# Softmax maxima sent out by halves of the queries, and the work of the last head pair laid out anew, in a DFT and attention kernel

## The chip, the cores and the metric

The kernel runs on one core of a Trainium2 chip. The metric is the device time of one execution in microseconds (us), the median of several runs. Inside the core, TensorE (PE) multiplies matrices, with weights loaded beside it (PEld); VectorE (DVE), ScalarE (ACT) and GpSimd (POOL) work elementwise and reduce; SyncE (SP) issues nearly all DMA transfers, in order.

## The reference

Two layers read the same input x of 2048 tokens by 640 features, and a gate of one number per token mixes them.

```python
a = x @ dft_hid_re.T ; b = x @ dft_hid_im.T
y = dft_seq_re @ a - dft_seq_im @ b                     # Fourier mixing
q = heads(x @ wq) ; k = x @ wk ; v = x @ wv             # 32 heads of 20, one k and v for all
p = softmax(q @ k.T * 20**-0.5)
o = (p @ v) @ wo
g = sigmoid((x * gate_w).sum(-1, keepdims=True))
out = g * y + (1 - g) * o
```

## The kernel before, in words

All operands are float32. Where accuracy asks for it an operand is split into a high and a low part and multiplied in three matmuls. The order on PE, ACT, DVE and POOL is the order in which the program issues (line 50, `manual_schedule`); SP's transfers are ordered by the framework.

**First stages (to 233 us).** q, k, v and the gate are projected. Then `x @ dft_hid` (line 137, tile `ab`) runs; its results `both` are stored to `x_d` in DRAM, while the first scores are already made. The operand tiles of this stage lie in two pools on the right side of SBUF, `w2` (the weights) and `x2` (inputs, `half`, `both`); both are closed before the main loop, whose pools (`cp`, `xp`, `pp` with the `pt` tiles, `op`) take their place.

**Attention.** Heads go in 16 pairs; each head of a pair uses one half of PE's rows, so two score matmuls of different halves run at the same time. Every score is made twice. An *a* score (line 353, 128 queries by 512 keys) serves the row maximum: DVE reduces it (line 360, tile `mx`). When the 64 units of a pair are done, `a_reduce` (line 366) and `a_final` (lines 374 to 376) reduce, transpose and split the maxima; they go to DRAM (`m_d`) and come back as rows 60 and 61 of each half of the query operand `qs`, where they subtract the maximum inside the matmul. A *b* score (line 811, 128 keys by 512 queries) uses that operand; ACT takes the exponential from PSUM into one of 16 `pt` tiles (line 821). An AV step (line 825, tile `av`) multiplies four `pt` tiles with the values; it fills all rows of PE. A b score of a pair needs that pair's maxima; a pair's b scores go by halves of the queries (`qh`), 16 key blocks each.

**DFT over the sequence.** One level of Strassen: 7 products, each of 8 blocks, 56 blocks in all; a block is 48 matmuls on each half of the rows (line 682, tile `y`, 320 columns). The matrix tiles are loaded as `craw` (1 MB for two), added where the product asks for it and split into `ch` and `cl` (lines 482 to 487, POOL, for the last blocks DVE). A block that ends is evicted by ACT (`y_evict`, line 711), then POOL adds it to earlier parts kept in `y_d`.

**The order by hand.** The string `PLAN`, *the list* below, is the main loop, one character for each step: `0` or `1` is a DFT matmul on that half of the rows; `a` to `f` and `A` to `F` are a scores of the pair's first and second head, and `g` to `l` and `G` to `L` b scores, where the letter names one of six PSUM banks; `V` is an AV step and `-` a DFT eviction. A score must wait until ACT or DVE has emptied its bank. The list holds 1,888 a scores (160 more came before it), 1,920 b scores, 4,608 DFT matmuls (48 blocks, accumulated in one bank, `GMAIN`, line 457) and 478 AV steps. `tick` (line 392) counts score pairs and starts what `later` set down.

**The last pair.** The loop from line 1025 on has 16 steps `kk`. Each runs 24 pairs of DFT matmuls, both halves at once into two banks, and four pairs of b scores of the last pair in a rotation of five banks; odd steps end with four AV steps (the first and the last step with two). Eight blocks are done there, each ending at the end of an odd step. Between the steps stand loads for the last stage (`BEFORE`: `load_wo` in steps 1 to 5).

**The end.** `o @ wo`, gated and added to y, from 1668 us on.

Of the kernel before, what the change touches and what calls it, by code (L numbers as in the profile page):

```python
# [34 lines left out]
def kernel(  # L35
# [46 lines left out]
    m_d = dram.tile([NPAIR, P, 2, 32], F32, name="m_d")  # L82
# [279 lines left out]
    mxr = {}  # L362

    def a_reduce(p):
        mxr[p] = sml.tile([P, 2 * NT], F32, name="mxr")
        nc.vector.tensor_reduce(
            mxr[p], mx.pop(p).rearrange("p h q c -> p (h q) c"), axis=AX.X, op=ALU.max
        )

    def a_final(p):  # L370

        mt = sml.tile([P, 32], F32, name="mt")
        ms = sml.tile([P, 2, 32], F32R, name="ms")
        nc.vector.transpose(mt, mxr.pop(p))
        nc.gpsimd.tensor_copy(ms[:, 0], mt)
        nc.gpsimd.tensor_tensor(ms[:, 1], mt, ms[:, 0].bitcast(F32), op=ALU.subtract)
        move(m_d[p], ms)

        m_v = m_d[p].rearrange("(g h b) i t -> h i b g t", g=4, h=2)
        for hh in range(2):  # L380
# [76 lines left out]
    GMAIN = LAST * NT // 5  # L457
# [3 lines left out]
    def load_c(g, sh):  # L461

        if g < len(GROUPS):
            n, k = GROUPS[g]
            c_raw[g, sh] = []
            for q, (i, th) in enumerate(PRODUCTS[n][0][::2]):
# [4 lines left out]
                move(raw, (cre, cim)[i][th * SJ + k, sh])  # L471
                c_raw[g, sh].append(raw)

    def split_c(g, sh):
        if g < len(GROUPS):
# [4 lines left out]
            eng = nc.vector if g > GMAIN else nc.gpsimd  # L480
# [387 lines left out]
    def finish_last(ts, sm):  # L868
# [20 lines left out]
        "B0A00K00F00CBjVV1e1g11d11l1c11h1e11a1j111f1h111c1-kJVHa1l1e11c1d11h11a1l11k1VHcDlAeVVCh1d1l11g1e11h1"
        "1c1l11d11gVHe0I0F00G0D00B0VIeGfDhVVhE0I0A00F00J000H0E00I00A0J000F0H00K00C0A00J0B00L00E0I000D0A000L0B"  # L890
        "iVVElj11c1g11b1l11e11d11i11g11h1l1e11c1-VdEaHcLVVDh1e1l11g1c11h111d1l11k1a111c1h11d111l1k1a1Hc1VLdKh"
        "AcVVfH0D0K00G0I00B00F0K00D0VVkAH00C00L0J00E0G00B00C00L00E0J000B00G0F00I00J00E00A0B0I00lDVVKc1a1l11h1"
        "1d1k11c1f11a111h11d1k11i1-VVBfKaIjVBk1i1f11j1a11k11h11c11l11d11a11k11h1c1f11d11KgVHkCfGdVVB00K00G0C0"
        "0L00D0B0K00G00I0F0D000E00B0A00LiVVDlI00E00H00A0L0J000C00E0H00A0L000C0D00BkVVFgIk1d111b1g11f11c1j111k"
        "1h111a1f11j1V-CaKbJlVk11c1j11a11l1h11e11c1d1GlV1e1h11c1g11d1l11e11b1iGVD0fIeB0A0VVJc0L0E000H0G00D00I"
        "00F0K00B0DgVVF00I00B0K00G0D00F00I00H0E00G00J00C0F00B0E000G0iJV1l1a11h1c11j11e11f1g11b1iDVVeGiFhJVe11"
        "fAi1b11j1-VIej11l11a111b1i1e111j1a1l11h11c1j11k11l1a11b1VcJaKlBVVdL0I0E00A0H00L00D0I00K0VViB0K0A0F00"
        "J00I00H00E0A000J0F0I00K00H00D00A000I0F00E0D00B0gCVV1f1g11e1j11b1i111l1a11k11d11i1h11f-AVVdKfIaHVdK1f"
        "1i11h11a11k1d1i11l111b1g11e1d11i11f1h111aKViDfBkAVViD00K0F00H0G00C0D00K0F000B0IaVViEJ00F0H00G00C0E00"
        "J0F00H000I00A000J0E00H0F00I00A0D00kHVVFh1c1g11e1j11b111l1a11i1j111e1l11h1VaE-cJfHVVaJ1e1h11i1l11d1g1"  # L900
        "11b11k1c1d111l1b11a111i11e1LjVIlBaDeVVlC0B0G00J0E0F00C00G0H00D0VVkA00L0B00I00D0Eg0L000B00I0D00G00K0F"
        "00C0H00G000J0K00F00B0CaVVj11f11k1b11i11a11j11lk111i11b1d11-GfVVKbIgDlVbKi11d11a11l1k11b11i1j111f1a11"
        "1k11b1i11d11l1eGVbDcFaKVVhED00I00L00A0H00E000I0J00L00B0A000I0E000J0H00F0aIVVjEF00H0A00I000J0E00H0F00"
# [99 lines left out]
    for what in PLAN:  # L1003
# [112 lines left out]
```

## Time and profile before

| | us |
|---|---|
| median of 3 runs | 1742.17 (1739.02 to 1743.29) |
| profiled execution | 1741.15 |
| its span, first to last instruction | 1739.4 |
| PE busy | 1727.9 |
| DVE busy | 1430.5 |
| ACT busy | 1195.5 |
| POOL busy | 815.4 |

The profile is of one execution. A row of a timeline has the start, the length, the engine, the line, the operation with tile written and tile read, the shapes and how many are merged; in brackets the idle time before it and what ended it. The ends of matmuls are modelled, so two lengths overlap; distances between starts are the safer reading. The chain of waits is followed back from the last instruction. A row of the windows has, for each engine, busy time and count, then the granted clock of PE as a share of full speed, the share of the DMA engines and GB/s.

### The profile page before, as it was taken

What the parts mean: (1) busy time and instruction counts of PE and PEld (TensorE: products, weight loads), DVE (VectorE), ACT (ScalarE), POOL (GpSimd) and SP (SyncE); (2) the same over time, 40 slices, a digit from 0 to 9 for tenths busy, and PEclk for the clock granted to TensorE, in tenths of its full rate; (3) what the DMA queues carried; (4) which work ended last, traced back from release to release, by engine and by line L of the source; (5) the groups of instructions that cost most, each with busy time, mean ns of one, the idle gap of its engine ahead of it and who ended that gap; (6) DMA issues with size and microseconds to landing.
All of it is one profiled execution on the core that took longest, in us unless ns stands there. A gap on an engine that the chain in (4) does not pass through costs nothing.

```text
span 1739.4 us, 40768 instructions
## 1 busy us (share of the span) xinstructions
PE 1727.9 (99%) x16342; PEld 1216.3 (70%) x16342; DVE 1430.5 (82%) x2355; ACT 1195.5 (69%) x2337; POOL 815.4 (47%) x559
## 2 busy tenths in 40 slices
PE   9999999999999999999999999999999999999999
PEld 8899976666666666666666666666666666667789
DVE  5779988888888898888898888889888898864254
ACT  4722257777777777777777777777777777777741
POOL 1012136554546464656666565565664344551242
PEclk9999999999999999999999999999999999999999
DMA  8873334243443442534544544253434233225667
GB/s 291 239 198 100 117 109 132 89 144 92 130 135 125 121 129 96 174 112 147 159 138 134 158 128 137 89 164 107 144 122 134 91 114 96 91 93 173 202 216 240
DMA packets 131002, 243.88 MB, mean 140 GB/s; under 512 B 26356, under 2 KB 77556, under 8 KB 128292
## 3 DMA queue, kind: packets, MB, share of 16 engines
q1 hardware_dynamic: 130012, 238.00, 43.6%
q0 software_dynamic: 800, 3.28, 0.6%
q8 instruction: 128, 2.10, 0.5%
q14 instruction: 62, 0.51, 0.1%
HBM read 194.62 MB, written 50.86 MB: 141 GB/s over the span
## 4 chain that ended last, share of the span: by engine, by line
PE 97%; DVE 1%; DMA 1%; ACT 0%; SPq 0%; issue 0%; ACTq 0%; DVEq 0%
PE av L825 28%; PE y L682 21%; PE b L811 17%; PE a L353 17%; PE ab L137 7%; PE o L126 1%; PE q L126 1%; PE q L128 1%; PE o L128 1%; PE o L127 1%; PE q L127 1%; DVE mx L360 1%; DMA x_d<-both 1%; DMA wqraw<-in_wq_dram 0%; PE kv L230 0%; PE kv L231 0%
## 5 line engine op out<-in xcount | busy, mean ns | idle before, releaser
L360 DVE TENSOR_REDUCE mx<-a 128x1 f32<-128x512 f32 x2048 | 1260.3, 681 | 159.4 <-PE a L353 101.4
L821 ACT ACTIVATE pt<-b 128x512 f32<-128x512 f32 x2048 | 1049.9, 621 | 319.4 <-PE b L811 191.1
L682 PE MATMUL y<-x,ch 64*128 64x320 f32 x3584 | 729.9, 304 | 1.1 <-ACT yt L711 1.1
L353 PE MATMUL a<-ks,qs 60*128 60x512 f32 x2048 | 723.2, 414 | 0.3 <-DVE mx L360 0.2
L811 PE MATMUL b<-qs,ks 62*128 62x512 f32 x2048 | 697.3, 415 | 2.0 <-ACT pt L821 1.7
L682 PEld LDWEIGHTS y<-x,ch 64*128 64x128 f32 x3584 | 551.2, 186 | 21.6 <-issue 10.5
L682 PE MATMUL y<-x,cl 64*128 64x320 f32 x1792 | 508.8, 304 | 0.0
L825 PE MATMUL av<-pt,vsb 128*32 128x512 f32 x4096 | 503.4, 600 | 0.0
L353 PEld LDWEIGHTS a<-ks,qs 60*128 60x128 f32 x2048 | 351.2, 185 | 140.2 <-DVE mx L360 102.5
L811 PEld LDWEIGHTS b<-qs,ks 62*128 62x128 f32 x2048 | 341.4, 185 | 141.7 <-ACT pt L821 72.7
L482 POOL TENSOR_TENSOR craw<-craw 128x1024 f32<-128x1024 f32 x80 | 189.4, 2368 | 267.0 <-DMA craw<-in_cre_dram 116.6
L682 PEld LDWEIGHTS y<-x,cl 64*128 64x128 f32 x1792 | 310.6, 186 | 3.5 <-issue 2.5
L825 PEld LDWEIGHTS av<-pt,vsb 128*32 128x32 f32 x4096 | 106.2, 109 | 194.6 <-issue 174.0
L487 POOL TENSOR_TENSOR cl<-craw,ch 128x1024 fp32r<-128x1024 f32 x98 | 231.9, 2367 | 7.8
L486 POOL CAST ch<-craw 128x1024 fp32r<-128x1024 f32 x98 | 101.6, 1037 | 142.2 <-PE y L682 113.6
L137 PE MATMUL ab<-wh,xh 64*128 64x320 f32 x640 | 126.6, 297 | 2.2 <-DVE both L557 1.8
L137 PE MATMUL ab<-wl,xh 64*128 64x320 f32 x640 | 126.2, 296 | 0.0
L137 PE MATMUL ab<-wh,xl 64*128 64x320 f32 x640 | 126.1, 296 | 0.0
L738 POOL TENSOR_TENSOR ya<-yt,ya 128x320 f32<-128x320 f32 x64 | 59.5, 946 | 97.8 <-ACT yt L711 93.9
L556 ACT ACTIVATE half<-ab 128x320 f32<-128x320 f32 x64 | 27.9, 436 | 104.1 <-PE ab L137 98.5
L137 PEld LDWEIGHTS ab<-wh,xl 64*128 64x128 f32 x640 | 92.9, 185 | 0.0
L137 PEld LDWEIGHTS ab<-wl,xh 64*128 64x128 f32 x640 | 92.9, 186 | 0.0
(88 smaller groups left out, 1083.3 us busy)
## 6 DMA issues: line engine op xcount, KB each, us to landing
craw<-in_cre_dram SPq DMA_DIRECT2D x96, 512.0 KB
craw<-in_cim_dram SPq DMA_DIRECT2D x96, 512.0 KB
xr<-x_d SPq DMA_DIRECT2D x88, 320.0 KB
qs<-qh_d SPq DMA_DIRECT2D x64, 160.0 KB
x_d<-both SPq DMA_DIRECT2D x64, 160.0 KB
ya<-y_d SPq DMA_DIRECT2D x64, 160.0 KB
y_d<-ya SPq DMA_DIRECT2D x64, 160.0 KB
xr<-in_xT_dram SPq DMA_DIRECT2D x20, 256.0 KB
```

Source lines behind the costliest of these rows:

```text
L126: nc.tensor.matmul(ps, wh, woven(xh), start=(i == 0), stop=False)
L137: nc.tensor.matmul(ps, w[r], woven(x[r]), start=(i == 0 and k == 0), stop=(i == n - 1 and k == 2))
L353: nc.tensor.matmul(ps, qs[p][b : b + 60, qb * P : (qb + 1) * P], woven(ks[b : b + 60, c * ROW : (c + 1) * ROW]), start=True, stop=True,)
L360: return nc.vector.tensor_reduce(mx[p][:, hh, qb, c : c + 1], ps, axis=AX.X, op=ALU.max)
L482: eng.tensor_tensor(raw, raw, raws[1], op=PRODUCTS[n][0][1])
L486: eng.tensor_copy(h, raw)
L487: eng.tensor_tensor(l, raw, h.bitcast(F32), op=ALU.subtract)
L682: mm = nc.tensor.matmul(ps[g % len(ps)], w, woven(x), start=start, stop=stop)
L738: nc.gpsimd.tensor_tensor(ya, yt, ya, op=how)
L811: nc.tensor.matmul(ps, ks[b : b + 62, kc * P : (kc + 1) * P], woven(qs[p][b : b + 62, qc * ROW : (qc + 1) * ROW]), start=True, stop=True,)
L821: halves.scored(nc.scalar.activation(t, ps, AF.Exp, scale=SCALE), n)
L825: nc.tensor.matmul(ps[32 * g : 32 * g + 32, :], vsb[:, kc, :], t, start=first, stop=last)
```

## The change

- **Maxima by halves.** `a_reduce` and `a_final` run after each 32 units, for 1024 queries, and send that half out: 32 stores to `m_d` in place of 16, and 128 loads into `qs` of half the size in place of 64. For the last pair the split is done by DVE in place of POOL.
- **The last half in the last pair.** The list ends with 32 units (64 a scores) left; steps 0 to 6 of the loop run them (`AS`), mixed with the b scores in the same five banks.
- **One more DFT block in the list** (`GMAIN` 49): 4,704 DFT matmuls there, 336 pairs in the loop, spread by `YS` over the steps; evictions come where a block of 48 pairs ends. c splits of four more blocks stay on POOL.
- **List, pools, load.** The list is another order, with 1,824 a scores, 1,920 b scores, 478 AV steps. Pool `x2` is allocated ahead of `w2`. The load of the first block's second half of c is issued by ACT. `load_wo` moves from steps 1 to 5 to steps 7 to 11.

```diff
-    m_d = dram.tile([NPAIR, P, 2, 32], F32, name="m_d")
+    m_d = dram.tile([2 * NPAIR, P, 2, 32], F32, name="m_d")
...
+    x2 = cw.enter_context(tc.tile_pool(name="x2", bufs=2, side="right"))
     w2 = cw.enter_context(tc.tile_pool(name="w2", bufs=1, side="right"))
-    x2 = cw.enter_context(tc.tile_pool(name="x2", bufs=2, side="right"))
...
-    mxr = {}
-
-    def a_reduce(p):
-        mxr[p] = sml.tile([P, 2 * NT], F32, name="mxr")
+    mxr = sml.tile([P, 2 * NT], F32, name="mxr", bufs=1)
+    nc.vector.memset(mxr, 0.0)
+
+    def a_reduce(p, f):
+
+        r = slice(SJ * f, SJ * f + SJ)
         nc.vector.tensor_reduce(
-            mxr[p], mx.pop(p).rearrange("p h q c -> p (h q) c"), axis=AX.X, op=ALU.max
+            mxr.rearrange("p (h q) -> p h q", h=2)[:, :, r], mx[p][:, :, r], axis=AX.X, op=ALU.max
         )
-    def a_final(p):
+    def a_final(p, f):
...
-        nc.vector.transpose(mt, mxr.pop(p))
-        nc.gpsimd.tensor_copy(ms[:, 0], mt)
-        nc.gpsimd.tensor_tensor(ms[:, 1], mt, ms[:, 0].bitcast(F32), op=ALU.subtract)
-        move(m_d[p], ms)
+        eng = nc.vector if p == LAST else nc.gpsimd
+        nc.vector.transpose(mt, mxr)
+        eng.tensor_copy(ms[:, 0], mt)
+        eng.tensor_tensor(ms[:, 1], mt, ms[:, 0].bitcast(F32), op=ALU.subtract)
+        m_p = m_d[2 * p + f]
+        move(m_p, ms)
...
+                move(row[:, r], m_v[hh, i : i + 1, r])
...
-        if u % 64 == 63:
-            later(1, a_reduce, u // 64)
-            later(2, a_final, u // 64)
+        if u % 32 == 31:
+            later(1, a_reduce, u // 64, u // 32 % 2)
+            later(2, a_final, u // 64, u // 32 % 2)
...
-    GMAIN = LAST * NT // 5
+    GMAIN = LAST * NT // 5 + 1
+    AMAIN = NA - 32
...
-                move(raw, (cre, cim)[i][th * SJ + k, sh])
+                move(raw, (cre, cim)[i][th * SJ + k, sh], nc.scalar if (g, sh) == (0, 1) else nc.sync)
...
-            eng = nc.vector if g > GMAIN else nc.gpsimd
+            eng = nc.vector if g > GMAIN + 3 else nc.gpsimd
...
-        "1aH1Id1k11f1a11h1111id1El11h1111i1g1Df1hKVDiG0B0F000KC00J00G0B00K0000F00J0C00gE0H00dFVVg11cHeD1lVgC0"
...
-        "0JkVVi11g11h1k11lJi1VVVj11i11g11111J11I11-"
...
+        "f1111k11c111j11gb111e1l1dVV00D0KF0000HA0I00J0E00000L000BI000G0J0E0000LB0C0V0F0BCjeG0VG0B0000ID0F000E"
...
+        "0H0000G0L00KH00I00G0000J0L0000000KHVVk1l11j111h1g111ik11VVVkiG11h1J111111I-"
...
-        **{kk: (lambda c=kk - 1: load_wo((c,)),) for kk in range(1, 1 + KC)},
+        **{kk: (lambda c=kk - 7: load_wo((c,)),) for kk in range(7, 7 + KC)},
...
-                if min(state) >= NA and sum(taken["b"]) % 2 == 0:
+                if min(state) >= AMAIN and sum(taken["b"]) % 2 == 0:
                     tick()
...
+    pairs = 0
+    AS = [5] * 6 + [2] + [0] * 9
+    YS = [19] * 7 + [23] * 5 + [22] * 4
     for kk in range(NT):
         block = 2 if kk in (0, NT - 1) else 4 * (kk % 2)
-        at = (1, 5, 9, 13) if block else (0, 6, 12, 18)
-        for i in range(24):
-            if i in at:
-                tick()
+        todo_s = sorted([((k + 0.25) / 4, 0) for k in range(4)] + [((k + 0.7) / AS[kk], 1) for k in range(AS[kk])])
+        span = YS[kk] - 6 if block else YS[kk]
+        for i in range(YS[kk]):
+            while todo_s and todo_s[0][0] * span <= i:
+                kind = todo_s.pop(0)[1]
+                if kind == 0:
+                    tick()
                 for g in range(2):
-                    next_b(g, f"S{lrot % 5}")
+                    tag = f"S{lrot % 5}"
                     lrot += 1
+                    if kind:
+                        waits(tag, -1)
+                        a_half(g, tag)
+                    else:
+                        next_b(g, tag)
             halves.run(0)
-            if i == 23:
+            pairs += 1
+            if pairs % (SJ * 6) == 0:
                 y_evict()
             halves.run(1)
-        y_evict()
+            if pairs % (SJ * 6) == 0:
+                y_evict()
```

More of the change, by code (lines that the diff above doesn't have):

```diff
@@ L889 @@
[L889 to L903, printed above, removed]
@@ L969 @@
[L969 to L973 removed]
+        "G1bc1je11L11g111b111j1111c1l11e1g111j1hlCVId0H0E0L000A0I0D000000HE000FG00IVkGfChJVVdHcgFKVg0DCK0000L"
@@ new lines @@
+        "B000000A0JEI0000FH0000J0G0C000K0000BDlV11f1h1d1k11111ia1l1b11111d1ki11a1111f-bVVF1a1h1ijEVIa11he1111"
+        "d11l1c111gb111k11l1j111a1ck11VkGCjbLVGC00000JH00F000EA0I000DVVjaIKbFVI000AK00B000F00JI0A00K000B000J0"
+        "F0000I0E000A0DH000I00FVVDg111lcb111k11g11111d1l1ck111h111ad-LVAHcefJVVEj111cl1111bgj1111e1l1c11111g1"
+        "1b1j111k1l1ac1VfGkBIdVE00H00I0D00000LA0E000H00J000CFA0000BVVAliJHeVi0A00EJ00L000BG0000I0D00E0000LBG0"
+        "00J0C00eFVVKc1f1111j11ha11i111e111jl1b11ac111-eJVV1ie1j1a111h11f1i11k1j1111a111hif1111k11a11dVaCkLDh"
@@ new lines @@
+        "Ve0GL00C0J0000H00AE00L00C00DVVJiFKbgV000CLK0B00000A0J0C0L00B00K00000J00GF00C0000E0B0J0lAVVbL11ge111j"
+        "11111c1hf11g111e1dc111h1lGVFjHeG-cVV1iGe1bLd1VgE1l111bdi11111g1e1111l1hi11j1111a1e1l1VDeIgLbVCjA0000"
+        "KB00L000J0000CE00GF00H00D0VV0J0FH00000E00G000I0DF0000HE00G0I0D000B000L0GVVBgl111d1c1k111a1h11111lj11"
+        "e11c1h11FgV-CbgKLdVV1dl1k1111b111a11i11dl1111h1k111cg1f11d1h11VbGjLEcVdH0K00F00I0G00B000D000K0F0CVVC"
+        "lkJaBVeIG0D000000H0FC00K00G00J0B0000F000K0C0000AH00D000KFVV111fj11a1k11hi11111f111dk1g1b111fVABe-jlI"
@@ new lines @@
+        "VDg11l11b11k1c11g11j11f1111h1e1c11aLjVf1iK11aJbV1Kg1c1hDfVVLb00DGI00000E0L0000HA00J0000C00K0L0A0000H"
+        "D00I00E00AVVg0C0K00B0JF000G00C00K0000HDVhE11d11i11gf1111h11ki1d11a11f1V1Acje1Bl1VV-KiFdhAVi111f111hd"
+        "111g1k1c1111f1h111dgei1111b111f1gVGe00H0C0D0F00000A0K0B0I0VV0A0H00C00L00K00DA000H000CL0000K0JB00A000"
+        "00F000CKhJV00FB0iEJgVbIjLe1a11VK1d1f1g11b1i111kj111g11f1c111b-VcgL1jK1b1VVKd11h1111fgc111kd11h11111f"
+        "g1111i1e11dh1VBkJcFgV0D00I0A0000LHE000DI000gFVD0GiF0K0000HVV00H0EI0000L00A000DH0E0I00F0000G0B0J0C000"
@@ new lines @@
+        "0K0GVVc1g111he11j1111lc111g111eb111j1c1VdB-gKcLVAj1k1h1cFVIe1bg1l1111d1111ika111h111f111d11c1g11eBfV"
+        "V000KB00IA00LJ0000E0B000C00000GLeJVVkjFiABV000JAI000H0F000K0D000A00IF00H000K00J00CA00H0VdCGheLVAjhc1"
+        "11k11l111d11a111h111ck111d11f-GbVVL1g1b1dCkV1a1kd111111i1hf111a11k11dc11h111lk11a1VcLkDAhVKc00DH00GF"
+        "00000EC0000HD00G0VVDiGEblV000GE0L0B00J0I00A0000K000FH0D00G000C0000ELH0000J0AVVGdh11111el111ca1111j11"
+        "h111kf1i111-daHVjiLE1b11aVVGfb1111ie1j111g111f1111ih11dk11g11l111cVaC000KFjHVdIeGFhVg0D0K00BL000C0G0"
@@ new lines @@
+        "0D000Eb000LC00AVVI0B00000KAL0D000I00H000K0A0F0000C000JB0g0K0VeGBiDlViE1hf111dg1111ie1111111bf111a11j"
+        "1iVVA-IldbKVi11f1j11bk11g111c11l111d111h11eg111c1f1j11bVVbLJ00C00A0K000F0H00000DI00K000AHVJk0AB00cLV"
+        "000KFH00C00GD00K000F00H00C0000G0ED000B00LVVd1K1111lb1ig11111d1el1111h1c1d11g1Va-CjH11le1VBIjgeFV1c1j"
+        "1e11l11111gb1c111jkf1111g11b1111dcVV00DI0BG000F0K000JC0000B000G0000K0LJC00G00B00E0VgBjCkFV0JcHK00fGV"
+        "fHe1c1J1gVk0Aj00F00IH00E00A0000DF00I0EhVVFhk11J111c1ah11f111k11c1d1111ghVaCJbeLVV-11h11f1k1cj111g11b"
@@ new lines @@
+        "11j1eb11l1111c1aKjVVa-JecHLV1b11kf1111i111g1d111k11bi111f1j11ae111h1i1VhAEIdlVIa0K0L0000D00H0CG0000E"
+        "0D00FVV00FJ000EGB000000IL0000DEG000I0000BF00D0G0V00ALb0C000KJVb11111jie11l1111ab1d111ck111l1g11VLjkB"
+        "cAV-VgECjbLVd1i1111f1h1111k1a1id111l1111b1ka111cd1111lV00CLA0000JK00B0000C0L0G0000DK000BF00000C0G000"
+        "JEVVKiDlAhVVh0F0AI0JK000000B0000F000GDC00HkV11b1i11e11j1al1111h1i1111e1j11f1aVJ-fcEgHVLd111a1i1h111e"
+        "l111d111ig11111be11l111d1cGbVV0IB00000JA0000KFI0H00000J0AK000CfVeIjGFbVd11lEg1BiVgEfJHcV0D00K0BL0000"
@@ new lines @@
+        "I00A0D00K000L0B0000I0000AE0L0D0HcVVj1111ch1111kf111a11jih111f1111-eGdV1eH1ljaC1V1a111j1fi1b1k111111g"
+        "11di11f11k1h11a11dVVJ000B00GE000LC0000J0B000AK00F0JiVAjEhFiVHa0Ki0D0LVVL0C0J000E0000G0BL0C0000J0000E"
+        "G00F0H000D0IVIf1b11j111k1a11if11d11h1e11111ac11Hf-VV1g1i1BkJfVhC1l1e1111dg111h1111cl1111k1g1d111b1cl"
+        "1VFHgjIeVVjA0C00K0B00L00D00A00K000I00F0HVbaCDLkVVi00EGDF000000H0I0K000A000J00HF0I0000A000KD00L00BVVh"
+        "F1d11k11i1g1111b1fk1111j1c111bg11-eFVVeHfAiJVC1k11l11d1g111be1111il11111d1a1c1bk1111l11jVCl0J0BK0000"
@@ new lines @@
+        "00GF0I0000D000BK0L0VbEfCJgVV000LA00IE00J00B000L0G00C00000K0DH00F0A000C00E0JhVVIbj11e11111al1111ib11j"
+        "1e111la1111chJVBgjE-IlVVi1Kdl1b1GV1e1lb111111gd1i111e1l111b1a1i111dl111kVgFE0000J0H00000CL0Aj000EH0C"
+        "000LVKhILdaVV0Lc0GB0J000K00000F0C00G00HD000LE0000A0I0B00000DFVVJb11gif1e1111j11h111a1f11i111e11d1GbV"
+        "VDgH-elCVBj11k1a111c1l11j11h1e11g11111fi1d11e1h1aLVf1kH1Gd1cVHdeLcAVVI0E00G00F00J000B0I0E0000G0F00J0"
+        "ChVhF000JI0000E0G0B0F000J00K000CH0000AD00L00E0I0VCjLaeHV111fg1111bkc111j111la11h111e1d11c-VVcJeHGfVh"
```

127 lines of the change are left out of this document (51 added, 76 removed).

## The prediction

> **What bounds the kernel now.** I read the page first (busy time, chain of waits), then the waits, then the timeline of each engine in three places: the start of the main loop, a steady stretch of it, and the last pair. From the page the span and its first part; below them two rows of the waits (engine, line, for whom: us in total, times, longest):
>
> ```profile
> span 1739.4 us, 40768 instructions
> PE 1727.9 (99%) x16342; PEld 1216.3 (70%) x16342; DVE 1430.5 (82%) x2355; ACT 1195.5 (69%) x2337; POOL 815.4 (47%) x559
> PEld a L353 <- DVE mx L360: 102.5, 146, 1.3
> PEld b L811 <- ACT pt L821: 72.7, 91, 1.9
> ```
>
> PE is never idle for long, so the time is the sum of what PE does; but its weight loads wait 102.5 us for DVE to free a score bank and 72.7 us for ACT. The change moves no matmul out of the kernel, so it can only alter waits. Durations are from an execution of 1741.15 us (span 1739.4), 1.0 under the median 1742.17; I apply the sum to the median. What a measurement here can tell from no change is 0.3%, 5.2 us: 1736.9 to 1747.4.
>
> Prices, from the timelines (start, length, engine, operation, count) of DVE, PE and ACT:
>
> ```profile
> 601.77 9.19 DVE L360 TENSOR_REDUCE mx<-a 128x1 f32<-128x512 f32 x15 [0.22 <-PE a L353]
> 601.22 0.48 PE L811 MATMUL b<-qs,ks 62*128 62x512 f32 x1
> 605.73 1.07 PE L825 MATMUL av<-pt,vsb 128*32 128x512 f32 x8
> 606.73 0.48 PE L811 MATMUL b<-qs,ks 62*128 62x512 f32 x1
> 609.77 1.07 PE L825 MATMUL av<-pt,vsb 128*32 128x512 f32 x8
> 611.62 1.92 PE L825 MATMUL av<-pt,vsb 128*32 128x512 f32 x16
> 613.47 0.48 PE L811 MATMUL b<-qs,ks 62*128 62x512 f32 x1
> ...
> 1578.17 0.38 PE L811 MATMUL b<-qs,ks 62*128 62x512 f32 x2
> 1578.39 0.30 PE L682 MATMUL y<-x,ch 64*128 64x320 f32 x2
> 1578.53 0.30 PE L682 MATMUL y<-x,cl 64*128 64x320 f32 x2
> 1578.58 4.03 ACT L821 ACTIVATE pt<-b 128x512 f32<-128x512 f32 x8
> ```
>
> A reduce costs DVE 9.19/15 = 0.613; an exponential costs ACT 4.03/8 = 0.504; a score holds its half of the rows 0.216 (1578.17 to 1578.39), a DFT matmul 0.136 (to 1578.53). One AV step takes 1.00 with what it costs to enter and leave (605.73 to 606.73), two 1.85 (611.62 to 613.47): 0.86 a step and 0.14 a group.
>
> **Start of the main loop (order of the two pools, and the load on ACT's queue).**
>
> ```profile
> 237.60 0.79 PE L811 MATMUL b<-qs,ks 62*128 62x512 f32 x1 [1.65 <-ACT pt L821]
> 236.95 3.98 ACT L821 ACTIVATE pt<-b 128x512 f32<-128x512 f32 x7 [3.03 <-DVE mx L360]
> 234.79 1.75 DMA x_d<-both
> 236.00:238.00 2.00, 0.40 (x2) 0.40 (x3) 1.15 (x2) 1.05 (x3) 0.00 (x0) 0.77 0.06 19
> 238.00:240.00 2.00, 2.00 (x13) 1.91 (x12) 0.66 (x2) 1.82 (x5) 0.00 (x0) 0.50 0.83 281
> 240.00:242.00 2.00, 2.00 (x13) 2.00 (x12) 0.63 (x2) 1.53 (x4) 0.96 (x1) 0.50 0.79 309
> 242.00:244.00 2.00, 2.00 (x12) 0.53 (x9) 1.29 (x2) 1.57 (x4) 1.94 (x2) 0.52 0.02 4
> 244.00:246.00 2.00, 2.00 (x20) 1.35 (x17) 1.11 (x2) 1.08 (x3) 1.92 (x2) 1.00 0.76 248
> ```
>
> The rows are PE's and ACT's timeline, the chain (start, length) and the windows, whose third number from the end is the granted clock. The first exponentials write `pt` tiles that lie where pool x2 had been; the chain has, where ACT's row names DVE, the last store out of `both`, which ends at 236.54, and only then does ACT run. PE stands 1.65 us, and after it the granted clock is 0.50 till about 243.9: 0.9 + 2 + 2 + 1.9 = 6.8 us at half speed, 3.4 lost. With x2 allocated first, `pt` takes w2's place, whose last readers are matmuls that PE has finished before any score of the loop. I take the whole 1.65 + 3.4 = **5.0** off. The load's two issues cost ACT some 0.7 us while it waits for scores anyway, so 0; without that cover the first exponential is 0.7 late. Bounds: 0 (something else holds `pt`) and 5.0.
>
> **The new list.** The groups of AV steps cut the list into sections. In a section PE issues scores faster than DVE and ACT empty six banks; during an AV group they catch up. So I count a section as the longest of three: the columns of its busier half; 0.613 for all reduces but two; 0.504 for all exponentials but two (one AV group of 1.00 hides 2.0 exponentials or 1.6 reduces). Try it on the section at 601.22, `Hc11k11a1l11d1h11c1k11a11l1j111b1e11c1l11a11j`, 9 + 9 scores and 27 DFT matmuls: columns 3.88, DVE 7 x 0.613 = 4.29; the trace has 4.51 (to 605.73). The next, `Lb0E0J00I0A00L0H00D000E00CgL0`: columns 2.60 against 3.04.
>
> ```profile
> 233.42 0.30 PE L682 MATMUL y<-x,ch 64*128 64x320 f32 x1
> 1570.27 0.29 PE L682 MATMUL y<-x,cl 64*128 64x320 f32 x1
> ```
>
> By that count the old list has 297 sections, 844.6 us (columns alone 751.5), 478 AV steps 411 and 296 groups 41: 1297. The loop took 1337 (233.42 to 1570.41), 1332 without the start's 5.0, so 0.12 a section stays over. The new list trades 64 reduces for 96 DFT matmuls (columns even) and cuts shorter: 345 sections, 344 groups; sections of 16 scores or more fall from 95 with 1,933 scores to 59 with 1,037, and those in which DVE or ACT is the longest from 176 to 123. Its sections count 807.8 (columns 764.0). So -36.8 in sections, +6.6 for 48 groups, +5.9 for what stays over: **-24.3**. Bounds: with three scores left over in place of two the sections count 769.9 and 767.7, 0.37 a section stays over, and the list costs -2.2 + 6.6 + 17.8 = +22; with 1.75, where nothing stays over, it gains 39. I take two, since that is what one AV group hides.
>
> **The last pair.** PE's own work stays: 48 DFT pairs fewer (-6.5), 32 score pairs more (+6.9): +0.4. Two waits are new.
>
> (1) DVE: in steps 0 to 5 of the loop ten reduces go with 19 DFT pairs. Even steps: columns 19 x 0.136 + 9 x 0.216 = 4.53, DVE 9 x 0.613 = 5.52; odd steps squeeze the scores into 13 pairs: 3.71 against 5.52. I leave one over, not two, because five banks serve here: 3 x (1.0 + 1.8) = +8.4 (+4.7 with two).
>
> (2) Block changes. Until now a DFT block ended right before an AV group, which hid the eviction of its banks:
>
> ```profile
> 1571.01 0.48 ACT L711 ACTIVATE yt<-y 128x320 f32<-128x320 f32 x1
> 1571.63 0.40 PE L682 MATMUL y<-x,ch 64*128 64x320 f32 x2 [1.07 <-ACT yt L711]
> 1582.34 3.57 PE av L825 x32
> 1582.43 0.51 ACT L711 ACTIVATE yt<-y 128x320 f32<-128x320 f32 x1
> 1582.77 0.50 ACT L711 ACTIVATE yu<-y 128x320 f32<-128x320 f32 x1
> 99.46 0.40 PE L137 MATMUL ab<-wh,xh 64*128 64x320 f32 x1 [1.75 <-DVE both L557]
> 50.00:110.00 60.00, 57.80 (x514) 52.79 (x514) 43.26 (x67) 36.35 (x57) 6.35 (x10) 1.00 0.77 218
> ```
>
> Now six changes of seven fall inside a step: after 48, 96, 144, 192, 240 and 288 pairs. The eviction is queued on ACT behind the exponentials already issued, the next block's first matmul waits for it, and everything behind that on PE too. Exponentials start 0.41 after their scores (1578.17, 1578.58), and PE goes on 0.62 after the eviction starts (1571.01, 1571.63). In step 9 three score pairs precede the change: 0.41 + 6 x 0.504 + 0.62 = 4.05, where PE arrives after 11 x 0.136 + 3 x 0.216 = 2.14: 1.9. Likewise step 11 (eight exponentials) 2.4, step 13 1.9, step 7 2.0, step 2 1.1, step 5 0.8: 10.1, and 0.34 each for the second bank (1582.43, 1582.77): 12.1. At the loop's start the list's end gives 2.2 by this working and gave 1.35 before (trace: 1.07): +0.8.
>
> Together **+21.7** (16 to 24).
>
> **The clock.** Five of these stalls last 1.9 us or more. In the rows one of 1.65 brought the half clock and one of 1.75 (99.46) did not. I take two of five; each costs 3.4, less 1.0 since ACT catches up while PE is slow and the next stall shrinks: **+4.8** (0 to 17). [...]
>
> **What costs nothing.**
>
> ```profile
> 1556.37 0.29 DVE L366 TENSOR_REDUCE mxr<-mx 128x32 f32<-128x128 f32 x1
> 1557.61 0.32 SPq L118 DMA_DIRECT2D m_d<-ms  x1
> 1559.06 2.51 SPq L118 DMA_DIRECT2D qs<-m_d  x4
> L487 POOL TENSOR_TENSOR cl<-craw,ch 128x1024 fp32r<-128x1024 f32 x98 | 231.9, 2367 | 7.8
> L486 POOL CAST ch<-craw 128x1024 fp32r<-128x1024 f32 x98 | 101.6, 1037 | 142.2 <-PE y L682 113.6 <-PE a L353 10.0 <-PE b L811 8.3
> ```
>
> The last maxima: reduce to last issue 5.2 us, landing about 1.4 more (the m_d write, 1557.61 to 1559.06), after 1.1 for the last score and its reduce: 7.7. From that score (step 6) to the first that needs it (step 8) PE has 0.3 + 3.4 + 2.0 + 3.7 + 0.3 = 9.7 us. Spare 2; uncovered it stalls PE by what is missing. Sixteen more round trips hold SP some 5 us each; behind them wait c loads and y loads, needed half a block (13 us) later. The doubled reduce and transpose add at most 2.6 to DVE. Eight c splits go to Pool at 1.0 + 2.4 = 3.4 each, two to a block of some 17 us: hidden, and else up to 3.4 each. load_wo on DVE waits till step 7, free of reduces, and wo is read after the pair.
>
> **Sum.** -5.0 - 24.3 + 21.7 + 4.8 = -2.8: 1742.17 - 2.8 = 1739.4.
>
> **Rivals.** *No half clock in the last pair*: for it the row at 99.46, against it that at 237.60; 1739.4 - 4.8 = 1734.6, 0.26. [...] *The list gains 39*, for it a lower count where DVE leads: 1724.7, 0.08. *Slower: the drains were hidden*, three scores can stay over, and 48 more AV groups are plain cost: -24.3 turns to +22, about 1786; for it the mere 175 us of waits on 1728 of PE, against it the section at 601.22; it decides from about 2.7 left over; 0.08. *Slower: the half clock at all five stalls*: three more at 3.4, 1749.6; above 1747.4 from the fifth stall on; 0.12. *The start's wait stays* (the pool order frees nothing): 1744.4, within the forecast's case.
>
> **Numbers.** The forecast, no change within 0.3%, has 0.46, own range 1736 to 1746. Faster 0.26 + 0.08 = 0.34, slower 0.08 + 0.12 = 0.20. The range for 8 in 10, 1728 to 1752, leaves out the list's extremes.
>
> **What would show it.** The row at 237.60 loses its 1.65 and the clock stays 1.00; the last DFT row of the list comes about 29 us earlier; both PEld waits shrink; in the last pair six rows "PE y <-ACT yt" stand with 1 to 2.4 us; it lasts about 25 us longer, with windows at 0.5 clock. I am wrong if the list's end moves less than 15 us, or the six rows are missing.

## The result, and the profile after

The kernel after takes 1765.06 us (median of 4 runs, 1763.88 to 1767.24), the kernel before 1740.94 (median of 4, 1739.02 to 1743.29). The ratio is 1.0136, with a 95% interval of 1.012 to 1.0152. It is slower by 24 us; the prediction had 1739.4 with a range of 1728 to 1752, and the one rival that ended far on this side had 1786. The profiled execution of after took 1763.88 us. Its page:

```profile
span 1762.1 us, 41047 instructions
PE 1738.7 (99%) x16342; PEld 1212.6 (69%) x16342; DVE 1428.3 (81%) x2376; ACT 1205.4 (68%) x2336; POOL 842.0 (48%) x602
```

PE is as full as before, over a span that is 22.7 longer. The waits of the weight loads for score banks (engine, line, for whom: us in total, times, longest) are spread otherwise:

```profile
PEld b L818 <- ACT pt L828: 67.1, 81, 3.2
PEld b L818 <- DVE mx L360: 62.6, 84, 1.1
PEld a L353 <- ACT pt L828: 55.5, 72, 0.9
PEld a L353 <- DVE mx L360: 53.7, 80, 0.9
```

Before, a scores waited 102.5 us for DVE and b scores 72.7 for ACT, 175 together; the two crossed rows were small then:

```profile
PEld b L811 <- DVE mx L360: 12.3, 31, 0.8
PEld a L353 <- ACT pt L821: 2.2, 12, 0.3
```

Now both kinds wait for both engines, and the four rows add up to 239 in place of 190. To see where the time went, I cut the span at three rows of PE's timeline: the start of the first DFT matmul, the end of the last one of the list, and the start of the first matmul of the last stage. They stand here for after, and the last of them for before (the other two of before stand in the prediction):

```profile
234.02 0.30 PE L689 MATMUL y<-x,ch 64*128 64x320 f32 x1
...
1563.37 0.30 PE L689 MATMUL y<-x,cl 64*128 64x320 f32 x1
...
1691.22 0.40 PE L126 MATMUL o<-wo,qs 128*128 128x320 f32 x1
```

```profile
1668.50 0.40 PE L126 MATMUL o<-wo,qs 128*128 128x320 f32 x1
```

| us | before | after | difference | predicted |
|---|---|---|---|---|
| to the first DFT matmul | 233.4 | 234.0 | +0.6 | 0 |
| the list | 1337.1 | 1329.6 | -7.5 | -29.3 (-24.3, and -5.0 at the start) |
| last pair, to the first o | 97.9 | 127.6 | +29.7 | +26.5 (21.7, and 4.8 of the clock) |
| the end | 70.9 | 70.9 | 0 | 0 |

The last pair is close to the forecast. The list is not: 22 of the 26 us by which the prediction is off lie there.

**The start.** Here stand a row of the chain (start, length), then ACT's and PE's timeline, then one of the windows (its third number from the end is the granted clock):

```profile
235.17 2.78 DMA x_d<-both
```

```profile
238.25 0.60 ACT L828 ACTIVATE pt<-b 128x512 f32<-128x512 f32 x1 [3.95 <-DMA x_d<-both]
238.27 0.38 ACTq L118 DMA_DIRECT2D craw<-in_cre_dram  x1
238.90 0.79 PE L818 MATMUL b<-qs,ks 62*128 62x512 f32 x1 [2.93 <-ACT pt L828]
```

```profile
238.22:245.04 6.82, 6.14 (x33) 5.24 (x37) 2.58 (x4) 5.13 (x10) 1.45 (x1) 0.50 0.44 155
```

The first exponential still waits for the last store out of `both` (it ends at 237.95). The stall is 2.93 us where it was 1.65, and the clock is halved behind it as before (0.50 from 238.22 on). The c load, now on ACT's queue, went out at 238.27, behind that exponential.

**Inside the list.** This is PE's timeline and, last, DVE's, right behind an AV group. In the list the place reads `VVi00AE0J`: a b score of the first half, two DFT matmuls of that half, then the a scores A and E of the other half.

```profile
1361.04 0.48 PE L818 MATMUL b<-qs,ks 62*128 62x512 f32 x1
1361.05 0.48 PE L353 MATMUL a<-ks,qs 60*128 60x512 f32 x1
1361.36 0.30 PE L689 MATMUL y<-x,ch 64*128 64x320 f32 x1
1361.37 0.38 PE L353 MATMUL a<-ks,qs 60*128 60x512 f32 x1
1361.50 0.29 PE L689 MATMUL y<-x,ch 64*128 64x320 f32 x1
1361.86 0.69 DVE L360 TENSOR_REDUCE mx<-a 128x1 f32<-128x512 f32 x1 [1.34 <-PE y L689]
```

Score A starts at 1361.05, ahead of the two DFT matmuls that stand before it in the program, and is done at 1361.53. Its reduce starts only at 1361.86, and the profile names as releaser not the score (L353) but a DFT matmul (L689), which ends at 1361.50 + 0.29 = 1361.79. In this trace the matmuls raise one counter of PE, and the reduce waits for it. By the times of its records it is raised in the order of the program and not of the starts: at 1361.53 (the b score), next at 1361.81 (the DFT matmuls), and only then at 1361.84 and 1361.88 (the two a scores). The reduce starts 0.02 after 1361.84. DVE had stood idle for 1.34 us, the last 0.3 of it for nothing. I counted such places by one criterion in every trace, from 250 us on (a reduce or exponential that starts with the end of an earlier listed matmul, and over 0.1 us after both its own score and its engine were ready). Before has none, after 126, which sum to 24.6 us (to within some ten places, since which record belongs to which score has to be inferred).

**The last pair.** PE's timeline; in brackets the idle time and what ended it. One row of the windows follows.

```profile
1565.77 0.44 PE L689 MATMUL y<-x,ch 64*128 64x320 f32 x2 [1.89 <-ACT yt L718]
1588.97 0.64 PE L689 MATMUL y<-x,ch 64*128 64x320 f32 x2 [0.68 <-ACT yt L718]
1609.57 0.64 PE L689 MATMUL y<-x,ch 64*128 64x320 f32 x2 [0.40 <-ACT yt L718]
1627.81 0.78 PE L689 MATMUL y<-x,ch 64*128 64x320 f32 x4 [1.70 <-ACT yt L718]
1635.05 0.45 PE L818 MATMUL b<-qs,ks 62*128 62x512 f32 x1 [0.84 <-DMA qs<-m_d]
1636.41 0.45 PE L818 MATMUL b<-qs,ks 62*128 62x512 f32 x1 [0.92 <-DMA qs<-m_d]
1645.82 0.73 PE L689 MATMUL y<-x,ch 64*128 64x320 f32 x2 [1.34 <-ACT yt L718]
1660.71 0.87 PE L689 MATMUL y<-x,ch 64*128 64x320 f32 x4 [2.01 <-ACT yt L718]
1676.70 0.87 PE L689 MATMUL y<-x,ch 64*128 64x320 f32 x4 [1.62 <-ACT yt L718]
```

```profile
1566.02:1569.42 3.40, 3.40 (x23) 3.40 (x23) 1.76 (x3) 1.98 (x4) 3.32 (x4) 0.50 0.29 100
```

The six block changes stand there, in steps 2, 5, 7, 9, 11 and 13, and the one at the loop's start. So do two waits that I had not forecast, for the last maxima (`qs<-m_d`, step 8). The trace's clock records have the half clock three times, at 1566.0, 1637.7 and 1661.6, for 3.413 us each; at the granted 0.50 PE does 0.5 x 3.413 = 1.7 us of work less in such a stretch. (The prediction's 3.4 came from the one at the start, 6.83 long.) Why the maxima were late is seen in DVE's and SP's rows:

```profile
1625.64 0.20 DVE L379 TENSOR_TENSOR ms<-mt,ms 128x32 fp32r<-128x32 f32 x1
1624.64 0.38 SPq L118 DMA_DIRECT2D rec_d<-rc  x1
1627.69 1.50 SPq L118 DMA_DIRECT2D rx_d<-rec_d  x2
1629.23 0.47 SPq L118 DMA_DIRECT2D m_d<-ms  x1
1630.84 1.14 SPq L118 DMA_DIRECT2D y_d<-ya  x2
1632.08 2.78 SPq L118 DMA_DIRECT2D qs<-m_d  x4
```

`ms` was there at 1625.84, but its store went out at 1629.23. Ahead of it on SP stood the round trip of the reciprocals of pair 14: the load of `rx_d` waits 2.6 us for the store to `rec_d` to land. Between the store and the loads stand a load of `wo` (1629.81) and y stores, which wait 0.7 us for POOL.

### The profile page after: what moved, and what is told of

Same layout as the page of the kernel before. It is cut to its first block, busy times and chain, and to the rows that moved or that the text cites. A ratio compares the mean times of both kernels' runs of the same rounds, so it can differ in the third digit from the quotient of the medians.

```text
span 1762.1 us, 41047 instructions
## 1 busy us (share of the span) xinstructions
PE 1738.7 (99%) x16342; PEld 1212.6 (69%) x16342; DVE 1428.3 (81%) x2376; ACT 1205.4 (68%) x2336; POOL 842.0 (48%) x602
## 4 chain that ended last, share of the span: by engine, by line
PE 94%; ACT 2%; DMA 1%; DVE 1%; issue 0%; POOL 0%; SPq 0%; ACTq 0%; POOLq 0%; DVEq 0%
PE av L832 28%; PE y L689 20%; PE b L818 16%; PE a L353 16%; PE ab L137 7%; ACT pt L828 2%; PE o L126 1%; PE q L126 1%; PE q L128 1%; PE o L128 1%; PE o L127 1%; PE q L127 1%; DVE mx L360 1%; DMA x_d<-both 1%; DMA ql_d<-ql 0%
## 5 line engine op out<-in xcount | busy, mean ns | idle before, releaser
L360 DVE TENSOR_REDUCE mx<-a 128x1 f32<-128x512 f32 x2048 | 1273.7, 682 | 211.3 <-PE a L353 137.4
L828 ACT ACTIVATE pt<-b 128x512 f32<-128x512 f32 x2048 | 1062.3, 610 | 333.8 <-PE b L818 212.3
L689 PE MATMUL y<-x,ch 64*128 64x320 f32 x3584 | 739.6, 304 | 9.6 <-ACT yt L718 9.6
L353 PE MATMUL a<-ks,qs 60*128 60x512 f32 x2048 | 717.2, 413 | 0.7
L818 PE MATMUL b<-qs,ks 62*128 62x512 f32 x2048 | 685.6, 413 | 4.9 <-ACT pt L828 2.9
L689 PEld LDWEIGHTS y<-x,ch 64*128 64x128 f32 x3584 | 563.5, 187 | 76.5 <-issue 43.4
L832 PE MATMUL av<-pt,vsb 128*32 128x512 f32 x4096 | 514.4, 602 | 0.0
L689 PE MATMUL y<-x,cl 64*128 64x320 f32 x1792 | 513.7, 301 | 0.0
L353 PEld LDWEIGHTS a<-ks,qs 60*128 60x128 f32 x2048 | 349.6, 185 | 117.5 <-ACT pt L828 55.5
L689 PEld LDWEIGHTS y<-x,cl 64*128 64x128 f32 x1792 | 322.8, 187 | 9.7 <-issue 9.2
L494 POOL TENSOR_TENSOR cl<-craw,ch 128x1024 fp32r<-128x1024 f32 x106 | 250.9, 2367 | 8.5
L832 PEld LDWEIGHTS av<-pt,vsb 128*32 128x32 f32 x4096 | 98.3, 109 | 184.5 <-issue 174.1
L493 POOL CAST ch<-craw 128x1024 fp32r<-128x1024 f32 x106 | 109.9, 1037 | 125.2 <-PE y L689 73.4
```

Source lines behind the costliest of these rows:

```text
L353: nc.tensor.matmul(ps, qs[p][b : b + 60, qb * P : (qb + 1) * P], woven(ks[b : b + 60, c * ROW : (c + 1) * ROW]), start=True, stop=True,)
L360: return nc.vector.tensor_reduce(mx[p][:, hh, qb, c : c + 1], ps, axis=AX.X, op=ALU.max)
L493: eng.tensor_copy(h, raw)
L494: eng.tensor_tensor(l, raw, h.bitcast(F32), op=ALU.subtract)
L689: mm = nc.tensor.matmul(ps[g % len(ps)], w, woven(x), start=start, stop=stop)
L818: nc.tensor.matmul(ps, ks[b : b + 62, kc * P : (kc + 1) * P], woven(qs[p][b : b + 62, qc * ROW : (qc + 1) * ROW]), start=True, stop=True,)
```

## The experiments

Times are medians; the ratio is to the kernel before on the same chip. For the stages of a run I cut the span of its profiled execution as above.

**Order inside the sections.** The sections and AV groups of the new list stay, each section's matmuls are put in the order in which PE was seen to start them. So the place shown above becomes:

```diff
-VVi00AE0J0B00000LI0G00D00E00LV
+VViA0E0J00B00L00I00G00D00E00LV
```

> After, with the matmuls of each section of the list put into the order in which the trace of after shows PE to start them (scores and DFT matmuls of one half keep their order, sections, AV groups and all counts stay). Theory L (late release): in after PE starts a score up to three matmuls ahead of its place in the list, but its reduce or exponential runs only when every matmul that stands ahead of the score has finished too; 140 drains of the list start 0.1 us or more late, 28 us in all over DVE and ACT. With the sorted list they start on time: list from 1329.5 to about 1320 us, time about 1756, ratio to before about 1.0085, late drains under 20. Rival S (the shorter sections cost more each by themselves, whatever the order inside): list and time stay, 1765 within 2 us.

Measured: 1750.99 (1745.61 to 1752.94, 5 runs), ratio 1.0047 (1.0032 to 1.0063). The list fell from 1329.6 to 1315.5 us, and late drains from 126 to 18 (the 140 and 28 us of the expectation were counted with a wider margin). The trace is of the execution of 1745.61, 5.4 under the median, and after's of one 1.2 under its own; so the stages differ by more in sum than the medians do. The same place, PE's and DVE's timeline:

```profile
1347.77 0.48 PE L818 MATMUL b<-qs,ks 62*128 62x512 f32 x1
1347.77 0.48 PE L353 MATMUL a<-ks,qs 60*128 60x512 f32 x1
1348.09 0.30 PE L689 MATMUL y<-x,ch 64*128 64x320 f32 x1
1348.09 0.38 PE L353 MATMUL a<-ks,qs 60*128 60x512 f32 x1
1348.23 0.29 PE L689 MATMUL y<-x,ch 64*128 64x320 f32 x1
1348.32 0.69 DVE L360 TENSOR_REDUCE mx<-a 128x1 f32<-128x512 f32 x1 [1.06 <-PE a L353]
```

PE does the same at the same distances. Only the reduce moved: 0.55 after its score's start in place of 0.81, and its releaser is the score. Rival S falls. The four rows of waits for score banks, by contrast, still add up to 236 us (239 in after), though the list is 14.1 shorter: they don't measure this loss.

**The opposite, in before.** The old list's scores are moved behind up to two DFT matmuls of the other half, as the new list writes them; for instance:

```diff
-Hc11k11a1l11d1h11c1k11a11l1j111b1e11c1l11a11j
+Hc1111k11a1l11d1h11c1k11a11l1j111b1e11c1l1a1j
```

> Before, with each score of the list moved behind up to two following DFT matmuls of the other half, which is how the new list writes them; sections, AV groups and counts stay. Theory L: the scores still start early, their drains come late, the list gets about 10 us longer: 1751, ratio about 1.006, with more than 100 drains late by 0.1 us or more (none in before). [...]

Measured: 1754.3 (1751.47 to 1756.75), ratio 1.0065 (1.0047 to 1.0083). The list grew from 1337.1 to 1348.3 us, with 82 late drains (over 100 were expected). So much order alone can do: 11 us, and more than that, since in this run the half clock at the start was missing, though PE had stood there for 1.62 us (PE's timeline and a window):

```profile
236.60 0.48 PE L811 MATMUL b<-qs,ks 62*128 62x512 f32 x1 [1.62 <-ACT pt L821]
```

```profile
237.00:244.00 7.00, 6.91 (x64) 5.19 (x62) 4.95 (x8) 6.80 (x15) 3.88 (x3) 1.00 0.59 194
```

**The start.** In the layout of after, `pt` tiles lie at 173,760 to 206,528 bytes of a partition and `x2` from 205,024 on. An overlap of 1.5 KiB, in the last `pt` tile alone, is enough: the framework frees a closed pool as a whole, and the first exponential, which writes a tile far from `x2`, carries waits for the transfers of `x2` (in the trace of after it waits for eleven counters, nine of them raised by DMA, the last at 237.95).

```diff
-    xp = ctx.enter_context(tc.tile_pool(name="xp", bufs=1))
     pp = ctx.enter_context(tc.tile_pool(name="pp", bufs=1))
+    xp = ctx.enter_context(tc.tile_pool(name="xp", bufs=1))
```

> After, with the pool of the pt tiles allocated ahead of xp, so that it ends below x2. As after lays out its tiles, the pt pool reaches 1.5 KiB into x2's place, and the first exponential waits for everything that used x2, the stores of both with it. Theory O (this overlap holds the first exponential): without it ACT starts the exponentials as soon as the scores are there, the stall of 2.93 us at 238.9 and the half clock behind it (6.83 us, 3.4 lost) go: about 6 us less, 1759, ratio about 1.010. Rival: something else of the closing pools holds ACT: start as in after, 1765, ratio 1.0136.

Measured: 1756.85 (1754.18 to 1758.45), ratio 1.0079 (1.0061 to 1.0096). The list took 1323.4, 6.2 less than in after. Of the windows, the one that was at half clock in after, and one in an earlier stage:

```profile
238.22:245.04 6.82, 6.82 (x71) 5.27 (x72) 6.10 (x11) 6.80 (x14) 3.48 (x3) 1.00 0.70 240
100.99:104.39 3.40, 3.40 (x29) 3.40 (x28) 0.34 (x1) 0.44 (x1) 0.00 (x0) 0.50 0.79 221
```

The stall and the half clock behind it are gone, so the rival falls. The other row is a half-clock stretch that this execution had and that of after had not; in return it had one in the last pair where after had three (the mean granted clock is 0.998, in after 0.995). Stretches come and go like this between kernels, at 1.7 us each, so single traces compare to some 2 to 5 us only.

The same repair in before, with `x2` ahead of `w2` as in the change and `pp` ahead of `xp`:

> Before with x2 allocated ahead of w2 and pp ahead of xp, nothing else: the start's repair alone. Theory O: the stall of 1.65 us at 237.6 goes, and the half clock behind it (6.83 us, 3.4 lost): 5 us less, 1736 to 1737, ratio 0.997. Rival (the first exponential has another late input, or scores then wait for DVE): 1741, ratio 1.000.

Measured: 1737.72 (1736.31 to 1740.82, 10 runs), ratio 0.9981 (0.9972 to 0.9991). The list is 4.5 shorter in the trace, the time 3.3 (1741.01 to 1737.72): the 5.0 of the prediction was an upper bound, and the change got none of it.

**Block changes.** Two AV steps move from a step's end to the change inside it (for the change in step 2, from the end of step 1):

```diff
+    EARLY = {48: 2, 96: 2, 144: 2, 192: 2, 240: 2, 288: 2}
...
-        block = 2 if kk in (0, NT - 1) else 4 * (kk % 2)
+        block = 2 if kk in (0, 1, NT - 1) else 4 * (kk % 2)
...
             if pairs % (SJ * 6) == 0:
                 y_evict()
+                for _ in range(EARLY.get(pairs, 0)):
+                    next_v()
+                if kk % 2:
+                    block -= EARLY.get(pairs, 0)
```

> After, with two of the AV steps of the last pair moved from the end of a step to each change of DFT block inside a step, where they run while the two banks are emptied. Theory C (the block changes inside the steps cost what PE is seen to wait there and what the clock does after it): PE's waits for yt in the last pair fall from 9.6 us to about 3, five more AV groups cost 0.7, one or two of the three half-clock stretches (3.41 us each) go: last pair 127.7 to about 118, time about 1756, ratio about 1.0085. Rival D (ACT and DVE are the bound of those steps, PE only waits where it is ahead): the waits move to the scores and AV steps, last pair 126 to 128, time 1764.

Measured: 1757.32 (1756.07 to 1757.73), ratio 1.0082 (1.0067 to 1.0097); the last pair 120.6 in place of 127.6. From the waits, in its last pair:

```profile
PE y L689 <- ACT yt L718: 2.1, 2, 1.9
PE b L818 <- DMA qs<-m_d: 3.0, 1, 3.0
```

The change's waits fell from 9.6 (seven times) to 2.1, of which 1.9 is the one at the loop's start. The wait for the maxima grew from 1.8 to 3.0: their loads went out 1.9 us earlier than in after (1630.21 on SP against 1632.08), but PE came to need them earlier by more. Rival D falls. Of theory C the part on the clock did not come: the last pair has one stretch of 3.41 us and one of 6.83 in place of three of 3.41, and the mean granted clock is 0.995 as in after.

**The reduces of the last pair.**

```diff
-        return nc.vector.tensor_reduce(mx[p][:, hh, qb, c : c + 1], ps, axis=AX.X, op=ALU.max)
+        part = ps[:, :P] if u >= AMAIN else ps
+        return nc.vector.tensor_reduce(mx[p][:, hh, qb, c : c + 1], part, axis=AX.X, op=ALU.max)
```

> After, where the 64 reduces of the last pair read 128 of their 512 columns (three quarters of the last half's maxima are left out, the scores are all computed). Theory V (these reduces hold back steps 0 to 5 of the last pair by the 8.4 us of the prediction's count): last pair 127.7 to about 119, time about 1757, ratio about 1.009. Rival H (they are hidden behind the matmuls and the waits for yt): last pair 127.7 within 1.5, time 1765, ratio 1.0136.

Measured: 1757.98 (1756.29 to 1759.83), ratio 1.0095 (1.0078 to 1.0112); the last pair 122.5. Steps 0 to 5, first in after, then in this run (windows; the third busy time is DVE's):

```profile
1565.77:1619.46 53.69, 52.02 (x449) 34.51 (x450) 36.79 (x60) 27.58 (x53) 23.52 (x18) 0.97 0.27 89
```

```profile
1565.10:1613.90 48.80, 47.66 (x448) 32.73 (x448) 14.64 (x60) 27.10 (x53) 23.55 (x18) 0.97 0.29 92
```

By the prediction's prices PE's own work in these steps is 114 x 0.136 + 54 x 0.216 + 14 x 0.86 + 4 x 0.14 = 39.8, so they stood 13.9 over it in after (1.3 in before). DVE's 22 us less took 4.9 of that away, not all.

**The last maxima.** Two changes: sent off at once, and the reciprocals ahead of them earlier.

```diff
-        if u % 32 == 31:
+        if u == NA - 1:
+            a_reduce(LAST, 1)
+            a_final(LAST, 1)
+        elif u % 32 == 31:
...
-            later(24, finish_sums, p, sm)
+            later(24 if p < LAST - 1 else 16, finish_sums, p, sm)
```

> After, with the last maxima sent off right behind their last reduce (two ticks earlier) and the reciprocals of the pair before last eight ticks earlier, so that their round trip no longer stands in front of the maxima on SP. Theory Q (SP's queue made the maxima late: ms was there at 1625.8, its store was issued at 1629.2 behind rec_d and rx_d, the last qs issue ended at 1634.9): the waits of PE for qs at 1635.05 and 1636.41 (0.84 and 0.92, and 2.2 of the weight loads) go, and with them the half-clock stretch at 1637.7: last pair 127.7 to about 124, time about 1761, ratio about 1.0115. Rival: the y stores that wait for Pool, behind its c splits, hold SP all the same: waits for qs stay at 3 to 4 us, time 1765.

Measured: 1760.2 (1758.53 to 1761.16), ratio 1.0107 (1.0092 to 1.0122); the last pair 125.5. SP's rows:

```profile
1625.16 0.32 SPq L118 DMA_DIRECT2D m_d<-ms  x1
1627.15 2.77 SPq L118 DMA_DIRECT2D qs<-m_d  x4
```

The loads went out 4.9 us earlier (0.8 of it since the list ended earlier), and PE's waits for `qs` are gone from the last pair. `ms` was ready at 1625.13, 0.7 earlier than in after, as the list's end is; so by these rows sending the maxima off at once moved nothing by itself, and the free queue did it: the store went out at once. Theory Q holds for the waits; the mean granted clock is 0.996 where after's is 0.995, and of the 3.7 us expected in the last pair 2.1 came.

**Maxima by halves alone, in before.**

> Before, with the maxima sent out by halves of the queries and nothing else changed. The prediction's claim N (the doubled reduce, transpose and round trip lie beside other work): ratio 0.9985 to 1.0015, list and last pair as in before, within 1.5 us each. Rival M (the sixteen round trips more hold SP's and Pool's queues and bring late loads, or the reduces hold DVE): 2 to 5 us longer, ratio 1.001 to 1.003.

Measured: 1742.17 (1739.88 to 1745.1, 11 runs), ratio 1.0002 (0.9994 to 1.0011); list 1335.5, last pair 97.9. The doubled round trips, reduces and transposes cost nothing that the time shows: by the interval 1.9 us at most. The list of this trace lacks the half clock at the start (3.4 us in before; the mean granted clock is 0.999, in before 0.998), so for its own work it is some 1.8 longer than before's, within what single traces tell apart.

**All repairs together**, and then the a scores of the last pair spread over whole steps:

> After with the sorted list, pp ahead of xp, AV steps at the block changes and the maxima of the run beside, together. If the costs are separate (14 us list, 6 to 8 start, 8 last pair, 4 maxima): about 1733, ratio 0.995. If they share waits and clock stretches: 1738 to 1745, ratio 0.998 to 1.002.

Measured: 1732.67 (1730.46 to 1734.53), ratio 0.9949 (0.9934 to 0.9964). That is the time expected for separate costs, and the kernel beats both. But the four single gains add up to 34.9 us by the medians and to 40 by the ratios, and 32 to 33 came together: the costs are separate for the most part, and a part of each is shared.

```diff
-    AS = [5] * 6 + [2] + [0] * 9
+    AS = [5, 6, 4, 6, 4, 6, 1] + [0] * 9
...
-[((k + 0.7) / AS[kk], 1) for k in range(AS[kk])]
+[((k + 0.7) / AS[kk] * YS[kk] / span, 1) for k in range(AS[kk])]
```

> The run with all four repairs, where in the last pair the score pairs of the maxima spread over a whole step instead of the 13 DFT pairs ahead of the AV steps, and steps that end with AV steps take six of them, the others four. Theory V (DVE falls behind in steps 0 to 5 because ten reduces come in 4.5 us, and AV time in which it could catch up is left unused): the steps 0 to 5, 12.6 us over PE's own work in that run, lose 4 to 6: time about 1728, ratio about 0.9925. Rival B (five banks shared with the exponentials are the bound, wherever the reduces lie): no gain over 1, ratio 0.9945 to 0.995.

Measured: 1728.04 (1725.63 to 1731.3), ratio 0.9924 (0.991 to 0.9939). Steps 0 to 5 in the run before it and in this one (windows):

```profile
1545.05:1597.66 52.61, 52.02 (x448) 33.55 (x449) 37.07 (x61) 27.58 (x53) 23.53 (x18) 0.97 0.29 96
```

```profile
1544.71:1591.84 47.13, 47.13 (x446) 33.34 (x446) 34.45 (x57) 27.49 (x53) 23.58 (x18) 0.96 0.30 100
```

PE's own work is 40.0 and 40.2 there, so 12.6 over it became 6.9 with 31 pairs of reduces in place of 30: their place in the step counts. Rival B falls. In step 11 about 2 us (1.10 at 1627.01 and 1.17 at 1628.72) were lost again, where PE waited for c splits on DVE. This is the fastest kernel of the study, 13 us under before.

## Why the prediction was wrong, step by step

**The list, -24.3: this step failed.** It came to -7.5, or -8.8 without the start's longer stall (1.3). The prediction took a section to last as long as its columns, its reduces but two or its exponentials but two, *by their counts*, and said so itself: "I count a section as the longest of three". That rule was fitted on the old list, in which no drain started late by the count above. It is blind to order: this is the term that was mis-sized. The new list writes DFT matmuls of one half in front of scores of the other that PE started first (1361.05 ahead of 1361.36), and 126 drains came late. The sum of the counts was about right: with the order mended and the same sections, the list is 14.1 shorter, and 8.8 + 14.1 = 22.9 stands against 24.3; its three terms were not measured apart. The prediction's own sign shows the failure too: it was wrong if the list's end moved less than 15 us, and the end moved 6.9 (1570.27 to 1563.37). I had both lists before me, and tried the rule on two sections of the old one only.

**The start, -5.0: wrong in where the tiles lie.** "`pt` takes w2's place" was reckoned from pool sizes, and the last tile reaches 1.5 KiB into `x2`. In place of -5.0 came +1.3 of stall, as the last store out of `both` took 2.78 us where it had taken 1.75 (why is open), and +0.6 to the first DFT matmul, which is within what the traces vary there (232.4 to 236.0). That the wait costs about this much, once it is really taken away, was right in size (6.2 in the list of after, 3.3 in the time of before). The rival "the start's wait stays" was the true one here.

**The last pair, +26.5 for +29.7: near in the sum, off in its terms.** The block changes were to be six, with 1.1, 0.8, 2.0, 1.9, 2.4 and 1.9; PE's rows have 0.68, 0.40, 1.70, 1.34, 2.01 and 1.62. The 0.34 more each for the second bank are not seen, so 7.8 stands against 12.1. The loop's start was to cost 0.8 more, and has 1.89 against 1.07. DVE was put at 8.4: steps 0 to 5 rose by 12.6 over their own work, less 1.7 of the clock and 1.1 of two changes, so 9.8. Shorter reduces took 4.9 of it away, and in a later run spreading them over the step, at full length, took 5.7; the two were not run together, so how far they are the same time is open. The half clock was put at 2 stretches with 4.8 in all; it was 3 of 1.7, 5.1: number and price were both off, and that they agree in sum is luck. What I missed are the maxima, given "spare 2": the working had nothing on SP between the last maximum and its store, and 3.4 us lay there, so PE waited 1.8 us on a path that was counted as free. With the 0.4 of PE's own work these terms make 25.7; some 4 us of the 29.7, in steps 6 to 15, stand in no row that I can name.

**What costs nothing** held otherwise: maxima by halves give 1.0002 by themselves, but the c load on ACT's queue went out 1.5 us later than on SP's (the load of `in_cim`: 238.68 against 237.20), and POOL's first add of c, which names that load as its releaser, began 2.55 us later (243.59 against 241.04). No wait of PE for it is seen.

**The sum.** The list missed by 15.5 (24.3 less 8.8), the start by 6.9 (5.0 + 0.6 + 1.3), the last pair by 3.2: 25.6, and 1739.4 + 25.6 = 1765.0. The slower rival, "the drains were hidden", had the right side by another way, 48 more AV groups as plain cost; those groups are all still there in the sorted list, which is 21.6 shorter than that of before, so that mechanism is out.

## What to carry to other kernels

- When an order is judged by counts, put next to them where each consumer is released. Here PE worked on two halves of its rows, and drains (a reduce or an exponential that empties a bank) went only after matmuls that were written ahead of their producer: 126 of them, 24.6 us in sum. With the matmuls written in the order in which PE was seen to start them 18 were left, and the list was 14.1 us shorter.
- A pool that overlapped a closed one by 1.5 KiB, in a single tile, waited for that pool's transfers (a stall of 2.93 us, gone in the run with `pp` first); look up addresses, not sizes.
- A short round trip whose working has room must have its queue looked at, row by row, for other round trips in front of it (here the store of `ms` went out 3.4 us after `ms` was there).

## What the runs showed of the hardware that I had not expected

- In the traces of before and after PE started matmuls out of program order where they use different halves of the rows, three places early at most; the rows at 1361 show a score that started at 1361.05, ahead of two DFT matmuls listed before it (1361.36 and 1361.50). The counter was raised in program order there all the same: at 1361.81 for the two DFT matmuls, at 1361.84 for the score.
- Whether a stall brought the half clock was not settled by its length: 1.65 us at 237.60 did in before, 1.62 at 236.60 in the clumped list did not, and in after 1.89 ahead of 1565.77 did (halved from 1566.0 on) where 1.70 ahead of 1627.81 and 1.62 ahead of 1676.70 did not. The clock records of before and after have all changes inside one trace at whole multiples of 3.413 us from each other: 6.83 at the start is two, and from the end of one half clock to the start of the next it is 387, 20 and 6 in after (1320.96, 68.27 and 20.48).
- In after's last pair the cases differ in how the stall lies to that spacing, carried through from the clock records. The 1.89 and the 2.01 (ahead of 1660.71) lie whole between two of its marks, and of the waits for the maxima 1.69 lie so; each time the half clock begins at the next mark (1566.0, 1661.6, 1637.7). The mark at 1627.45 cuts the 1.70 into 1.34 and 0.36, the one at 1675.23 the 1.62 into 0.15 and 1.47, and the clock stays at 1.00. Earlier stages do not follow this: in before the 1.75 ahead of 99.46 lie whole between 97.13 and 100.54 and the clock stayed at 1.00, while 1.37 between 233.66 and 237.07 had the half clock behind them.

So a stall of 1.6 to 2 us had the half clock behind it in some places and not in others, which a count of the work alone does not tell. What decides it is not shown; no run shifted a stall on purpose.
